# A decode layer on one core: PV with V as the stationary operand, whole last loads, and the FFN weights behind V

## The chip, the core and the metric

The kernel runs on one core of a Trainium2 chip. The metric is device microseconds (us) for one execution of the program. The engines named below are PE (TensorE matmul; PEld is its weight load), DVE (VectorE), ACT (ScalarE), POOL (GpSimd) and SP (SyncE, which here only issues DMAs). All DMAs of the core are carried out by 16 DMA engines.

## The reference

Two tokens (B = 2, one position each, D = 512) go through one transformer layer: attention over a cache of 8,192 positions with 32 heads of 128, and then a gated feed-forward network of width 1,376. Everything is bf16.

```python
def _A_ref(x, k_cache, v_cache, wq, wo):          # attention, 32 query and 32 KV heads
    q = (x @ wq).reshape(B, Sq, Hq, Dh).transpose(0, 2, 1, 3)
    scores = jnp.einsum("bhqd,bhkd->bhqk", q, k) * (Dh ** -0.5)
    p = _softmax(scores, axis=-1)
    o = jnp.einsum("bhqk,bhkd->bhqd", p, v)
    return o.transpose(0, 2, 1, 3).reshape(B, Sq, Hq * Dh) @ wo

def _B_ref(x, W_gate, W_up, W_down):
    gate = jnp.einsum("bsd,df->bsf", x, W_gate)
    up = jnp.einsum("bsd,df->bsf", x, W_up)
    gate = gate * (gate > 0)
    return jnp.einsum("bsf,fd->bsd", gate * up, W_down)

h = x + _A_ref(_layernorm(x), A_k_cache, A_v_cache, A_wq, A_wo)
h2 = h + _B_ref(_layernorm(h), B_W_gate, B_W_up, B_W_down)
```

The two caches are 2 x 32 x 8192 x 128 each, 134 MB in bf16, and every byte of them is read once: 268 MB of the 281 MB that the kernel loads.

## The kernel before

**Tiles.** The 64 (token, head) problems are worked on in NP = 32 pairs p of two heads of one token. For a pair, K is one tile of 128 partitions (two heads of 64) by J = 128 positions by 128 numbers, 4 MB in one transfer with 32 KB a row; V is the same. Four slots of that size hold K[p], V[p], K[p+1], V[p+1]; pair p's K is in slot 2p mod 4 and its V in slot 2p+1 mod 4.

**Scores of a pair** (loop at L399). Of the 128 positions of a partition, 96 are scored on DVE, in two parts c of 48: a product with the broadcast query (L407, 3.36 us), four halving additions (L415) and a reduction (L424). The other 32 are scored on PE: in four groups of eight they are transposed (L434) into one of two PSUM tiles Tp, copied to SBUF by ACT (L440), and multiplied with the query (L274). ACT makes the exponentials of the three pieces (L282) and their sums zs.

**PV of a pair** (`pv`, L341). For p < 31 the exp weights are the stationary operand: 8 columns (4 positions by 2 heads) are loaded, and 4 positions of V, 512 wide, move past them; 32 such matmuls (L361) sum into a bank of Op, in four groups of rows. `collect` (L368) then copies the bank to `os_sb` with ACT (L372) and picks the wanted pieces with four fp32 matmuls against a selection matrix `sel` into the bank `Ob` (L378; the trace shows each fp32 matmul as two). For the last pair V is the stationary operand, 128 by 128, and 2 columns of exp weights move (L354, 128 matmuls).

**Normalization.** After pairs 7, 15, 23 and 30, `z_sum` (L295) adds zs over partitions on PE, and `normalize` (L300) makes sums, reciprocals and the scaled O_sb on DVE. Batch 3 (pairs 24 to 30) is normalized in the middle of pair 31's DVE work (L418). Batch 4 is pair 31 alone.

**The end.** After the loop: `o_proj` (L328) of heads 24 to 31 that are ready, z_sum of batch 4, PV of pair 31, its scaling (`o_scale`), the last output projection, the layer norm, the two FFN input products (L518), their gate on DVE, the FFN output product (L560) and the result's DMA. These stand in a fixed order in each engine's program.

**Order of the work.** It is written by hand: every engine runs its instructions in program order, and waits on semaphore counts. All large loads are issued from SP's queue in this order: wq, K0, V0, K1, V1, the last rows of W_down, wo, then K[p+2] as soon as pair p has read its K (`t_kfree`), and V[p+2] as soon as PV of pair p is done. At the end the order is K30, K31, V30; then, when K30's slot is free, W_up and W_gate into it, V31 in four transfers of 1, 1.5, 1.25 and 0.25 MB with a semaphore each (`vparts`), and W_down. PE waits for both of W_up and W_gate at L512 and for all of W_down at L554.

## Time and profile before

| | us |
|---|---|
| time, median of 3 runs | 672.62 (672.58 to 673.44) |
| the profiled execution's own time | 672.58 |
| its span | 670.7 |
| PE busy, 3,868 matmuls | 352.0 |
| DVE busy | 494.4 |
| ACT busy | 220.1 |
| read from HBM | 281.05 MB, 419 GB/s over the span |
| DMA engines, packets of the data queue | 98.4% of the span |

Times in the profile run from the start of the span. The page gives busy time for each engine, the span in 40 slices with the busy share of each in tenths, the DMA queues, and the costliest groups of instructions with their source line (L12 is line 12). The chain that ended last follows the work back from the last instruction, at each step to what released it. The timeline lists instructions by time; a row with "x8" is eight merged instructions. A queue of the kind "instruction" carries the fetches of an engine's program, and one of the kind "hardware_dynamic" the kernel's own transfers. The trace also holds every DMA packet with queue, start, duration and size.

### The profile page before, as it was taken

Reading aid. Unit: us, or ns where it says so; the run is one execution under the profiler, and the core shown is the slowest. Engines: PE = TensorE matmul, PEld = TensorE weight load, DVE = VectorE, ACT = ScalarE, POOL = GpSimd, SP = SyncE. Lnnn points to the kernel's source line nnn. Section 1 sums busy time; section 2 is a strip of 40 time slices with the busy share of each in tenths; the row PEclk is TensorE's granted clock in tenths of the full one; section 3 lists DMA queues with packets and bytes.
Section 4 is the critical chain, followed back from the end, with each engine's and each line's share of the span. In section 5 each row is a group of like instructions: output and inputs, shape, how many; then the busy total and the mean of one; then the engine's idle time right before and its main releaser. Section 6 shows DMA issues by size and latency. Waiting matters only on the chain.

```text
span 670.7 us, 8986 instructions
## 1 busy us (share of the span) xinstructions
PE 352.0 (52%) x3868; PEld 234.1 (35%) x3868; DVE 494.4 (74%) x430; ACT 220.1 (33%) x554; POOL 2.5 (0%) x16
## 2 busy tenths in 40 slices
PE   2553355455545455554554655454556565455655
PEld 2431333233433223343322433232234443223435
DVE  1774477788768678877777887677786977678792
ACT  0631322233432234344222333322333342233340
POOL 1000000000000000000000000000000000000000
PEclk9999999665565555655556656655566555565555
DMA  9999999999999999999999999999999999999994
GB/s 375 434 436 357 434 435 430 427 431 429 434 433 427 428 433 433 425 436 425 434 433 427 431 436 424 431 432 431 437 426 425 434 432 433 426 430 431 428 409 146
DMA packets 15915, 281.63 MB, mean 420 GB/s; under 512 B 1442, under 2 KB 6916, under 8 KB 7044
## 3 DMA queue, kind: packets, MB, share of 16 engines
q1 hardware_dynamic: 15872, 281.06, 98.4%
q8 instruction: 30, 0.49, 0.3%
q14 instruction: 9, 0.07, 0.0%
q10 hardware_dynamic: 4, 0.00, 0.0%
HBM read 281.05 MB, written 0.00 MB: 419 GB/s over the span
## 4 chain that ended last, share of the span: by engine, by line
DMA 72%; DVE 22%; PE 3%; ACT 2%; issue 1%; SPq 0%; DVEq 0%
DMA slot<-in_A_k_cache_dram 68%; DVE prod L407 14%; DVE tb L415 4%; DMA slot<-in_A_v_cache_dram 3%; DVE prod L415 2%; ACT kT L440 1%; DVE scores L424 1%; PE T L434 1%; PE Ob L378 1%; ACT e L282 0%; PE S L274 0%; ACT os_sb L372 0%; PE Ob L295 0%; PE S L518 0%; PE O L560 0%
## 5 line engine op out<-in xcount | busy, mean ns | idle before, releaser
L407 DVE TENSOR_TENSOR prod<-slot,q_b 128x6144 bf16<-128x6144 bf16 x64 | 214.9, 3358 | 128.2 <-DMA slot<-in_A_k_cache_dram 126.9
L361 PE MATMUL O<-slot,e 128*8 128x512 bf16 x992 | 116.3, 621 | 143.4 <-ACT e L282 127.8
L440 ACT ACTIVATE kT<-T 128x1024 bf16<-128x1024 bf16 x128 | 126.2, 1021 | 160.2 <-PE T L434 159.4
L434 PE MATMUL T<-ident,slot 128*128 128x128 bf16 x1024 | 122.0, 305 | 65.3 <-DMA slot<-in_A_k_cache_dram 65.3
L415 DVE TENSOR_TENSOR tb<-prod 128x3072 bf16<-128x3072 bf16 (+1 forms) x128 | 148.2, 1158 | 4.4
L434 PEld LDWEIGHTS T<-ident,slot 128*128 128x128 bf16 x1024 | 99.3, 140 | 92.3 <-DMA slot<-in_A_k_cache_dram 90.6
L282 ACT ACTIVATE e<-scores 64x48 bf16<-64x48 f32 x128 | 32.8, 256 | 239.2 <-DVE scores L424 237.6
L361 PEld LDWEIGHTS O<-slot,e 128*8 128x8 bf16 x992 | 24.0, 106 | 209.6 <-ACT e L282 155.6
L415 DVE TENSOR_TENSOR prod<-tb 128x1536 bf16<-128x1536 bf16 (+1 forms) x128 | 84.2, 658 | 4.4
L378 PE MATMUL Ob<-sel,os_sb 128*128 128x2 f32 x248 | 57.5, 354 | 47.7 <-ACT os_sb L372 47.7
L378 PEld LDWEIGHTS Ob<-sel,os_sb 128*128 128x128 f32 x248 | 54.9, 327 | 51.2 <-ACT os_sb L372 51.2
L274 PE MATMUL S<-qT,kT 128*128 128x2 bf16 x1024 | 48.2, 168 | 39.2 <-ACT kT L440 38.1
L274 PEld LDWEIGHTS S<-qT,kT 128*128 128x128 bf16 x1024 | 40.7, 106 | 57.5 <-ACT kT L440 57.5
L424 DVE TENSOR_REDUCE scores<-prod 128x48 f32<-128x384 bf16 x64 | 35.4, 553 | 2.2
L282 ACT ACTIVATION_READ_ACCUMULATOR e<-scores 64x1 f32 x128 | 23.6, 185 | 0.0
L372 ACT ACTIVATE os_sb<-O 128x512 f32<-128x512 f32 x31 | 18.5, 597 | 3.4 <-PE O L361 2.7
L282 ACT ACTIVATE e<-S 64x32 bf16<-64x32 f32 x64 | 12.9, 202 | 15.0 <-PE S L274 14.2
L282 ACT ACTIVATION_READ_ACCUMULATOR e<-S 64x1 f32 x64 | 12.8, 201 | 0.7
L251 ACT ACTIVATE q_b<-O 128x512 bf16<-128x512 f32 x8 | 4.3, 595 | 15.8 <-PE O L246 15.8
L222 DVE CAST qT<-W 128x64 bf16<-128x64 f32 x1 | 0.2, 224 | 12.2 <-PE W L217 12.2
L217 PE MATMUL W<-xlT,X 128*128 128x2 bf16 x128 | 3.6, 166 | 8.8 <-DMA X<-in_A_wq_dram 8.8
L217 PEld LDWEIGHTS W<-xlT,X 128*128 128x128 bf16 x128 | 3.5, 104 | 8.8 <-DMA X<-in_A_wq_dram 8.8
(67 smaller groups left out, 58.8 us busy)
## 6 DMA issues: line engine op xcount, KB each, us to landing
slot<-in_A_k_cache_dram SPq DMA_DIRECT2D x32, 4096.0 KB, 27.7
slot<-in_A_v_cache_dram SPq DMA_DIRECT2D x31, 4096.0 KB, 31.3
X<-in_A_wq_dram SPq DMA_DIRECT2D x1, 4096.0 KB, 12.5
X<-in_A_wo_dram SPq DMA_DIRECT2D x1, 4096.0 KB, 48.7
slot<-in_A_v_cache_dram SPq DMA_DIRECT2D x1, 1536.0 KB, 19.8
slot<-in_B_W_up_dram SPq DMA_DIRECT2D x1, 1376.0 KB, 10.0
slot<-in_B_W_gate_dram SPq DMA_DIRECT2D x1, 1376.0 KB, 14.6
slot<-in_A_v_cache_dram SPq DMA_DIRECT2D x1, 1280.0 KB, 22.2
```

The costliest lines, as they stand in the source:

```text
L217: i = nc.tensor.matmul(Wp[:, h * B:(h + 1) * B], lhsT=wq[:, c, h * Dh:(h + 1) * Dh], rhs=lT[:, c * B:(c + 1) * B], start=(c == 0), stop=(c ...
L251: t_cp[m] = act.run(nc.scalar.activation(out=q_b[:, m * 512:(m + 1) * 512], in_=Op[m % 2][:], func=ACT.Copy))
L274: i = nc.tensor.matmul(Sp[p % 2][:, 2 * jj:2 * jj + 2], lhsT=kT[n % 3][:, k * 128:(k + 1) * 128], rhs=qT[:, 2 * p:2 * p + 2], start=True, ...
L282: t = act.run(nc.scalar.activation(out=e_t[p % 2][q, j0:j0 + nj, a], in_=src(q, a), func=ACT.Exp, scale=inv_sqrt_dh, accum_out=zs[q, 2 * p ...
L361: i = nc.tensor.matmul(o[g:g + 2 * VJ, :], lhsT=e_t[p % 2][:, j:j + VJ, :].rearrange("p j a -> p (j a)"), rhs=v_t[:, j:j + VJ, :].rearrang ...
L372: t_os[p] = act.run(nc.scalar.activation(out=os_sb[:], in_=Op[p % 2][:], func=ACT.Copy))
L378: i = nc.tensor.matmul(Ob[:, 2 * p:2 * p + 2], lhsT=os_sb[:, jj * Dh:(jj + 1) * Dh], rhs=sel[:, 2 * jj:2 * jj + 2], start=(jj == 0), stop= ...
L407: t_dm = dve.run(nc.vector.tensor_tensor(out=prod[:], in0=k_t[:, c * JC:(c + 1) * JC, :], in1=qv, op=ALU.mult))
L415: dve.run(nc.vector.tensor_tensor(out=o, in0=cur[:, :, 0:half], in1=cur[:, :, half:w], op=ALU.add))
L424: t_s = dve.run(nc.vector.tensor_reduce(out=sc[:], in_=cur, axis=AX.X, op=ALU.add))
L434: i = nc.tensor.transpose(Tp[n % 2][:, k * 128:(k + 1) * 128], k_t[:, j, :], ident[:])
L440: t_ev[n] = act.run(nc.scalar.activation(out=kT[n % 3][:], in_=Tp[n % 2][:], func=ACT.Copy))
```

## The change

The source is shorter by 49 lines. What it does:

- `pv` has one form for all pairs: 128 matmuls with V stationary and 2 columns of exp weights moving, straight into the pair's two columns of a bank of Op, which belongs to its batch. `collect`, `os_sb`, `sel`, the bank `Ob` and the zeroing of Op at the start are gone; z_sum follows the last PV of a batch and uses column 64 on of the same bank.
- The freed bank becomes a third transpose tile Tp.
- `pv(30)` and `normalize(3)` move behind the loop; before, they stood in the middle of pair 31's work on PE and DVE.
- V31 is one transfer, issued ahead of W_up and W_gate; W_up and W_gate have a semaphore each, and W_down comes in two parts (six and four blocks of 128 rows) with a semaphore each. PE waits for each where it needs it.

```diff
-    VJ = 4
+    WD_PARTS = ((0, 6), (6, 10))
...
-        Tp = [ps(f"T{i}", [128, GT * 128], BF16) for i in range(2)]
+        Tp = [ps(f"T{i}", [128, GT * 128], BF16) for i in range(3)]
...
-        Ob = ps("Ob", [128, 512], F32)
...
-                dve.wait(t_cp[NP // 4 - 2], t_cp[NP // 4 - 1])
-                for o in Op:
-                    t_zero = dve.run(nc.vector.memset(o[:], 0.0))
...
                 def zbank(k):
-                    return Sp[0] if k == 4 else Ob
+                    return Sp[0] if k == 4 else Op[k % 2]
...
                 def pv(p):
                     v_t = tile((2 * p + 1) % 4)
-                    o = Op[p % 2]
-                    parts = vparts if p == NP - 1 else (
-                        [(0, NCH * JC, J)] + [(1 + c, c * JC, (c + 1) * JC) for c in range(NCH)])
-                    pe.wait(t_zero)
-                    if p >= 2:
-                        pe.wait(t_os[p - 2])
+                    k = next(kk for kk, (a, b_) in enumerate(batches) if a <= p < b_)
+                    col = 2 * (p - batches[k][0])
+                    parts = [(0, NCH * JC, J)] + [(1 + c, c * JC, (c + 1) * JC) for c in range(NCH)]
+                    if p == batches[k][0] and k >= 2:
+                        pe.wait(t_O[k - 2])
                     nmm = 0
...
-                        for j in range(j0, j1, VJ):
-                            g = 32 * (nmm % 4)
+                    for ei, j0, j1 in parts:
+                        pe.wait(t_exp[p][ei], t_v[p])
+                        for j in range(j0, j1):
                             i = nc.tensor.matmul(
-                                o[g:g + 2 * VJ, :], lhsT=e_t[p % 2][:, j:j + VJ, :].rearrange("p j a -> p (j a)"),
-                                rhs=v_t[:, j:j + VJ, :].rearrange("p j d -> p (j d)"),
-                                start=(nmm < 4), stop=(nmm >= J // VJ - 4))
+                                Op[k % 2][:, col:col + 2], lhsT=v_t[:, j, :], rhs=e_t[p % 2][:, j, :],
+                                start=(nmm == 0), stop=(nmm == J - 1))
                             nmm += 1
                     t_pv[p] = pe.run(i)
-
-                def collect(p):
-                    act.wait(t_pv[p])
...
-                    t_os[p] = act.run(nc.scalar.activation(out=os_sb[:], in_=Op[p % 2][:], func=ACT.Copy))
...
-                    for jj in range(VJ):
-                        i = nc.tensor.matmul(
-                            Ob[:, 2 * p:2 * p + 2], lhsT=os_sb[:, jj * Dh:(jj + 1) * Dh],
-                            rhs=sel[:, 2 * jj:2 * jj + 2], start=(jj == 0), stop=(jj == VJ - 1))
-                    t_ob[p] = pe.run(i)
-                    if p + 1 in ends:
+                    if p + 1 in ends and p < NP - 1:
                         t_batch[k] = z_sum(k, *batches[k])
...
-                            if p == NP - 1 and c == 1 and w == Dh // 2:
-                                t_O[3] = normalize(3, 24, 31, t_batch[3], False)
...
-                                if n >= 2:
-                                    pe.wait(t_ev[n - 2])
+                                if n >= 3:
+                                    pe.wait(t_ev[n - 3])
...
-                            if p == NP - 1:
-                                pv(p - 1)
-                            if p >= 1:
-                                collect(p - 1)
...
                     elif p == NP - 2:
 
+                        load_v(p + 1)
                         sp.wait(*t_kfree[p])
                         for k, w in enumerate((B_W_up, B_W_gate)):
                             nc.sync.dma_start(
                                 slot[0][:, k * DC * F:(k + 1) * DC * F],
-                                w.rearrange("(p c) n -> p (c n)", c=DC)).then_inc(sem_w, 16)
-                        load_v(p + 1, vparts)
+                                w.rearrange("(p c) n -> p (c n)", c=DC)).then_inc(sem_w[k], 16)
+                        for k, (r0, r1) in enumerate(WD_PARTS):
+                            nc.sync.dma_start(
+                                slot[0][:, 2 * DC * F + r0 * D:2 * DC * F + r1 * D].rearrange("p (r n) -> p r n", n=D),
+                                B_W_down[r0 * 128:r1 * 128].rearrange("(r p) n -> p r n", p=128)).then_inc(sem_wd[k], 16)
...
+                pv(NP - 2)
+                t_O[3] = normalize(3, 24, 31, t_batch[3], False)
                 pe.wait(t_O[3])
                 o_proj(range(HM, 30), 0, 2)
...
-                pe.wait((sem_w, 32), t_d)
+                pe.wait(t_d)
...
+                pe.wait((sem_w[0], 16))
                 t_u = ffn_in(Sp[1], wup, 0, FC)
+                pe.wait((sem_w[1], 16))
                 t_g = (ffn_in(Op[1], wgt, 0, FH), ffn_in(Wp, wgt, FH, FC))
...
-                pe.wait((sem_wd, 32))
+                pe.wait((sem_wd[2], 16))
                 for k, (f0, f1) in enumerate(((0, FH), (FH, FC))):
-                    pe.wait(t_hd[k])
+                    pe.wait(t_hd[k], (sem_wd[k], 16))
```

## The prediction

> **What bounds the kernel now.** I read the page first, engines, slices and queues; then the chain that ended last, in order of time; then the timeline of the last 50 us; then the trace's DMA packets one by one.

> ```profile
> PE 352.0 (52%) x3868; PEld 234.1 (35%) x3868; DVE 494.4 (74%) x430; ACT 220.1 (33%) x554; POOL 2.5 (0%) x16
> DMA  9999999999999999999999999999999999999994
> q1 hardware_dynamic: 15872, 281.06, 98.4%
> q8 instruction: 30, 0.49, 0.3%
> L361 PE MATMUL O<-slot,e 128*8 128x512 bf16 x992 | 116.3, 621 | 143.4 <-ACT e L282 127.8
> L378 PE MATMUL Ob<-sel,os_sb 128*128 128x2 f32 x248 | 57.5, 354 | 47.7 <-ACT os_sb L372 47.7
> ```

> No compute engine is full; the DMA engines are, in every slice but the last. The kernel streams 281 MB, and K[p] and V[p] are 4 MB each. The fourth row will matter: 30 instruction fetches on a queue of their own, which use the same 16 DMA engines.

> The chain shows the beat at which K tiles arrive (start, length, what; DVE starts when K lands):

> ```profile
> 388.25 3.37 DVE prod L407
> ...
> 428.14 3.37 DVE prod L407
> ...
> 467.00 3.37 DVE prod L407
> ...
> 545.24 3.37 DVE prod L407
> ...
> 585.12 3.37 DVE prod L407
> ...
> 623.98 3.37 DVE prod L407
> ```

> Two pairs (four transfers) take 38.86 us, 9.715 us a transfer, except now and then: 388.25 to 428.14 is 39.89, 545.24 to 585.12 is 39.88. Something adds about 1 us to the slowest engine.

> The tail is the timeline (start, busy, engine, line):

> ```profile
> 652.36 0.19 DVE L303 TENSOR_REDUCE zr<-Ob 128x14 f32<-128x42 f32 x1
> 653.09 1.15 PEld L328 LDWEIGHTS W<-O_sb,X 128*128 128x128 bf16 x32 [1.59 <-DVE O_sb L316]
> 655.05 0.55 DVE L424 TENSOR_REDUCE scores<-prod 128x48 f32<-128x384 bf16 x1
> 656.38 0.50 PEld L295 LDWEIGHTS S<-zs,ones_f 128*128 128x128 f32 x2 [2.14 <-ACT e L282]
> 656.61 2.40 PEld L354 LDWEIGHTS O<-e,slot 128*128 128x128 bf16 x80
> 659.34 1.44 PE L354 MATMUL O<-e,slot 128*128 128x2 bf16 x48 [0.25 <-DMA slot<-in_A_v_cache_dram]
> 660.89 0.16 DVE L316 TENSOR_TENSOR O_sb<-O,zi 128x2 bf16<-128x2 f32 x1 [3.52 <-PE O L354]
> 662.41 1.53 PE L518 MATMUL S<-d_b,slot 128*128 128x2 bf16 x44 [0.34 <-DVE d_b L503]
> 665.24 1.48 PE L560 MATMUL O<-hd,slot 128*128 128x2 bf16 x40
> ```

> So the end is set twice, nearly at once: K30's landing (623.98) plus 31.6 us of uninterrupted DVE for pairs 30 and 31 gives the last scores at 655.60; and the last quarter-megabyte of V31 lands at 659.3. From 660.89 (o_scale) the rest is a fixed 9.8 us.

> **The steady state: instruction fetches.** The 30 packets of q8 have 16,384 bytes each. PE and PEld have 7,736 records, 258 a fetch, and the n-th fetch starts when the trace has passed about 256n of them (fetch 26 at 608.4 us, after 6,661): this queue feeds PE. Each 4 MB transfer leaves 16 completion writes of 4 bytes in the trace, one for each DMA engine. First and last of them for some transfers:

> ```
> first engine   last engine   lag     PE fetch just before
>    121.59        123.94      2.35    119.96 (5th)
>    218.71        222.11      3.40    215.71 (9th)
>    315.84        319.78      3.94    314.58 (13th)
>    412.97        417.95      4.98    407.91 (17th)
>    500.53        505.90      5.37    500.71 (21st)
>    578.24        584.65      6.41    578.24 (25th)
>    617.09        623.50      6.41    (this is K30)
> ```

> Engines that fetch nothing keep the 9.715 us beat. After a fetch one engine falls back by 1.53 to 1.56 us and never recovers, since all engines have a queue ahead of them. At K30 the 16 lags are six under 0.6, two at 2.8 and 4.0, six at 4.58 to 5.39 and two at 6.23 and 6.41. With 1.54 a hit, that is 6 x 3 + 2 x 4 = 26 hits, just the 26 fetches begun by then: they go round 8 engines. A transfer counts as landed when its slowest engine is done, so the worst-hit engine sets K30.

> What the change adds: for each of 31 pairs 128 matmuls in place of the 32 of L361 and the 8 of L378 (248/31), so 31 x 88 = 2,728 pairs of weight load and matmul; PE goes from 3,868 to 6,596 pairs, from 30 fetches to about 51. Up to K30's landing: 168 pairs of the prologue, 29 x 192, 64 of pair 29's transposes and scores, some 130 of its PV and 6 of z sums, about 5,936 pairs or 11,870 records: 46 fetches for 26. Round 8 engines 46 makes six engines with 6 hits and two with 5. The worst before has 4 hits and a lag of 0.25 besides (6.41 - 6.16); of the engines with 3 hits one has 0.77 besides (5.39 - 4.62), and by its turn (5th, 13th, ... 45th) it gets its sixth hit in time. New lag 6 x 1.54 + 0.77 = 10.0: K30 lands **3.6 us later**. Bounds: the first engine's two more hits alone 3.1; an average of 20 more fetches over 8 engines 3.85; a seventh hit on one engine 5.1 (9.24 + 0.77 + 1.54 - 6.41); nothing, if the extra fetches fall on engines with room. I take 3.6, as it follows the same count that closes before.

> [...]

> **The rest of the steady state costs nothing.** PV of one pair on PE: 32 wide matmuls took 3.58 us (timeline, 645.00) and the L378 group 1.87; 128 narrow pairs at 2.40/80 = 30 ns take 3.84. ACT loses the 0.60 us copy of L372. PE's total of about 9.2 us a pair lies under a beat of 19.4. K[p+2] is issued 11.1 us after K[p] lands (604.54 to 615.68), V[p+2] after pv(p), some 18 us after, with three transfers of 9.7 us still queued, so neither delay is seen. At the three batch ends normalize now follows pv(p) directly: exps end 16.1 us after K's landing, 48 pairs 1.4, z_sum 0.6, three DVE operations 0.8, done at 19.0 of 19.4. The start drops two memsets (1.03 us, L257) and POOL's copies, covered by K2, which is not issued before 35.96 and then waits in the queue. PE's third transpose bank only loosens a wait.

> **The tail, step by step, relative to K30.** normalize(3) leaves the middle of pair 31's DVE work (the gap 652.45 to 653.07, less the usual 0.03: -0.59), so the last scores come at 655.01. It now runs behind them, 0.68 us (652.36 to 653.04), ready 655.69; queued behind it on DVE is only normalize(4), while PE's o_proj and everything after wait for it. 32 o_proj pairs (1.15 us) start 655.74; z_sum's first load to PV's first is 0.23 (656.38 to 656.61), so PV31 loads from 657.1. All 128 pairs now stand behind this point: 3.84 us, matmuls done about 661.05. Before, they ended 660.78. That is **+0.27**: the wait for V31's last part goes, and 48 more pairs plus o_proj come in its place. At the nearest slower row (L274: 8 in 0.38, 47 ns, pipeline fill included) it would be +2.4; at the prologue's 3.57/128 = 28 ns under a granted clock of 1.00, against 0.50 in the tail, about -0.3 over PV and FFN. I keep L354's own 30 ns. pv(30), moved behind pair 31's scores (done 645.1), needs 3.84 us and a z_sum, over by 650 at the old time, 5 us before normalize wants it.

> DMA order: V31 goes ahead of W_up and W_gate as one issue for four, W_down as two for one. V31's wait for pv(29) (done 622.2) now stands in SP's queue ahead of the wait for K30's slot (635.11), so it holds nothing back. V31 lands at 633.70 (K31) + 2 x 9.715 + 3.6 = 656.7, needed at 660.7. The weights then take 3.26, 3.26 and 3.04 us at 432 GB/s: 660.0, 663.2, 666.3 against uses at 666.3, 667.7 and 669.1. Same bytes, nothing late. The split waits on PE thus all fall on landed data.

> **Sum:** profiled execution 672.58 (span 670.7, 1.9 around it) + 3.6 + 0.27 = 676.45, +0.57%. The median of the runs shown is 672.62, the same within 0.04, so **676.4**.

> **Rivals.** (A) The fetches do not move K30: hidden, or dealt out over other engines in the longer program. Price +0.27 alone: **672.9**, not slower within what can be told (0.2%, 1.35 us, is about what a measurement of this kernel can tell from no change). It decides as long as K30 lands before 625.1. For: the prologue of the ring is not in the trace, and a fetch is only 0.3% of the DMA time. Against: 26 hits counted out of 26 fetches. Faster would need over 1.6 us from landings; a spread over 16 engines (3 hits for 4) would give 1.0 less, 671.9. (B) One more turn: a seventh hit, or the same worst engine also takes an 8 KB fetch of the other engines' queue (9 in the run, 0.7 to 1.0 us each): K30 +5.1, **678.0**; the weights' slack of 2.8 us is then nearly used as well, and past it W_down's second part, now the last transfer, sets the end. For: PE's burst of some 300 pairs in the tail draws three or four fetches there. Against: the count of 46. (C) PE as the new bound, with 128 weight loads a pair at 47 ns, 6.0 us: still 11.4 of 19.4 a pair, but +2.4 in the tail, 672.58 + 3.6 + 2.4 = **678.6**. Against: L354 has 128 of these very pairs.

> **How the numbers follow.** Forecast 0.74, A 0.12, B and C together 0.14. The likeliest gives 676.4. The range runs from 674.5 (one hit less on the worst engine, 3.6 - 1.54 = 2.1, and the tail's +0.27 taken back by the faster row) to 678.6 (C, with B inside); A stays outside. Slower: forecast, B and C, 0.88, less a little for hits that miss K30, 0.86; A gives 0.10 of no change and 0.04 of faster.

> **What would show it.** The q8 row with about 51 packets; lags of first to last engine of about 10 us at K30; the first prod of pair 30 at 627.6; the base beat still 38.86 per two pairs; o_scale of the last batch 36.9 to 37.3 us after K30's landing; no wait of PE for V31 or a weight. Wrong, if q8 grows and K30 stays at 624, if PV31 spaces its pairs over 35 ns, or if PE stalls on its own instructions.

## The result, and the profile after

The changed kernel takes 676.11 us (median of 4, 675.81 to 676.30) where the kernel before takes 672.79 (median of 4): a ratio of 1.0047 with an interval of 1.003 to 1.0065, slower by 3.3 us. The profiled execution took 675.94 us with a span of 674.2, against 672.58 and 670.7.

The page of the changed kernel, its engines, its slices and its DMA queues:

```profile
PE 294.7 (44%) x6596; PEld 266.7 (40%) x6596; DVE 493.6 (73%) x428; ACT 202.2 (30%) x523; POOL 1.7 (0%) x11
DMA  9999999999999999999999999999999999999993
q1 hardware_dynamic: 15456, 281.06, 97.9%
q8 instruction: 51, 0.84, 0.5%
L333 PE MATMUL O<-e,slot 128*128 128x2 bf16 x4096 | 118.5, 165 | 236.9 <-ACT e L268 119.0
```

PE is less busy than before (294.7 us for 352.0), and so is ACT. The bytes are the same. What has grown is the row that looks like nothing: 51 instruction fetches for 30, and PE's count of pairs, 6,596 for 3,868.

The chain in order of time, as before with the first product of every second pair (start, length, what):

```profile
429.71 3.37 DVE prod L359
...
470.11 3.37 DVE prod L359
...
508.95 3.37 DVE prod L359
...
549.33 3.37 DVE prod L359
...
588.18 3.37 DVE prod L359
...
627.01 3.37 DVE prod L359
```

The undisturbed beat is the same: 508.95 - 470.11 = 38.84, 588.18 - 549.33 = 38.85. The long steps are 40.40 and 40.38, 1.5 us over the beat. By the last completion writes of the 4 MB transfers from V4 to K30 there are five such steps, of 1.4 to 1.55 us, where the kernel before has six, of 0.5 or 1.0: they are not more frequent but larger. Pair 30 starts at 627.01 instead of 623.98.

The timeline of the tail (start, busy, engine, line):

```profile
657.49 0.55 DVE L374 TENSOR_REDUCE scores<-prod 128x48 f32<-128x384 bf16 x1
657.96 0.19 DVE L286 TENSOR_REDUCE zr<-O 128x14 f32<-128x42 f32 x1
658.69 1.15 PEld L310 LDWEIGHTS W<-O_sb,X 128*128 128x128 bf16 x32 [6.83 <-DVE O_sb L298]
660.00 3.68 PEld L333 LDWEIGHTS O<-e,slot 128*128 128x128 bf16 x128
663.87 0.16 DVE L298 TENSOR_TENSOR O_sb<-O,zi 128x2 bf16<-128x2 f32 x1 [3.11 <-PE O L333]
665.29 0.50 PE L467 MATMUL S<-d_b,slot 128*128 128x2 bf16 x13 [0.26 <-DVE d_b L452]
666.22 1.18 PE L467 MATMUL S<-d_b,slot 128*128 128x2 bf16 x31 [0.42 <-issue]
668.70 1.48 PE L511 MATMUL O<-hd,slot 128*128 128x2 bf16 x40
```

From K30's landing to o_scale it is 663.87 - 627.01 = 36.86 us, before 36.91: the tail neither gained nor lost there. No wait for V31 or for a weight is left. But the FFN's 44 matmuls, one run before, are cut in two: PE stands still at 665.6, for "issue", that is for nothing the profile shows. From o_scale to the FFN's output product it is 4.83 us instead of 4.35. So the 3.46 us by which the last DVE operation is later (670.43 against 666.97) are 3.03 from K30, -0.05 from the attention's tail and 0.48 from the FFN.

### The profile page after: what moved, and what is told of

Same layout as the page of the kernel before. It is cut to its first block, busy times and chain, and to the rows that moved or that the text cites. A ratio compares the mean times of both kernels' runs of the same rounds, so it can differ in the third digit from the quotient of the medians.

```text
span 674.2 us, 14429 instructions
## 1 busy us (share of the span) xinstructions
PE 294.7 (44%) x6596; PEld 266.7 (40%) x6596; DVE 493.6 (73%) x428; ACT 202.2 (30%) x523; POOL 1.7 (0%) x11
## 3 DMA queue, kind: packets, MB, share of 16 engines
q1 hardware_dynamic: 15456, 281.06, 97.9%
## 4 chain that ended last, share of the span: by engine, by line
DMA 70%; DVE 27%; PE 2%; issue 1%; SPq 0%; DVEq 0%
DMA slot<-in_A_k_cache_dram 70%; DVE prod L359 16%; DVE tb L367 6%; DVE prod L367 4%; DVE scores L374 2%; PE O L333 1%; PE S L467 0%; PE W L310 0%; PE O L511 0%; SPq L136 0%; PE W L467 0%; PE O L467 0%; PE S L278 0%; SPq L152 0%; DVE O_sb L298 0%
## 5 line engine op out<-in xcount | busy, mean ns | idle before, releaser
L333 PE MATMUL O<-e,slot 128*128 128x2 bf16 x4096 | 118.5, 165 | 236.9 <-ACT e L268 119.0
L333 PEld LDWEIGHTS O<-e,slot 128*128 128x128 bf16 x4096 | 114.4, 104 | 241.1 <-ACT e L268 121.5
L260 PE MATMUL S<-qT,kT 128*128 128x2 bf16 x1024 | 48.3, 168 | 38.6 <-ACT kT L390 37.3
L310 PE MATMUL W<-O_sb,X 128*128 128x2 bf16 (+1 forms) x136 | 5.0, 172 | 7.0 <-DVE O_sb L298 7.0
L310 PEld LDWEIGHTS W<-O_sb,X 128*128 128x128 bf16 x136 | 4.8, 118 | 7.2 <-DVE O_sb L298 7.2
```

The costliest lines, as they stand in the source:

```text
L260: i = nc.tensor.matmul(Sp[p % 2][:, 2 * jj:2 * jj + 2], lhsT=kT[n % 3][:, k * 128:(k + 1) * 128], rhs=qT[:, 2 * p:2 * p + 2], start=True, ...
L310: i = nc.tensor.matmul(Wp[:, c * B + b0:c * B + b1], lhsT=wo_m[:, h, c, :], rhs=Ov[:, h // 2, h % 2, b0:b1], start=first[0], stop=last, sk ...
L333: i = nc.tensor.matmul(Op[k % 2][:, col:col + 2], lhsT=v_t[:, j, :], rhs=e_t[p % 2][:, j, :], start=(nmm == 0), stop=(nmm == J - 1))
```

## The experiments

They ran in two sets, each on one chip and beside the kernel before: new order alone, old order, 91 and 182 matmuls more beside a median of 673.03 us, the other four beside 672.91. The ratios are to these medians. Two questions stood open: is it the number of PE's instructions, or the narrow weight loads of V, or the new order of the last loads; and what bounds the tail.

### The order of the last loads alone

```diff
-                        pe.wait(t_exp[p][ei], (sem_vl[ci], 16) if p == NP - 1 else t_v[p])
+                        pe.wait(t_exp[p][ei], t_v[p])
...
+                        load_v(p + 1)
                         sp.wait(*t_kfree[p])
...
-                        load_v(p + 1, vparts)
```

> The kernel before with one part of the change alone: V31 as one transfer ahead of W_up and W_gate; PV stays 512 wide. Fetch theory: PE's program is the same, so 30 fetches, lag at K30 6.4 us, first prod of pair 30 at 624.0. PV31 no longer waits for V31: 128 pairs at 29 to 30 ns behind 656.6, o_scale at 660.4 to 660.6 for 660.89, so 672.2 to 672.4 us. Rival (the new order of the last loads is what costs): 675.5 to 676.5 us.

Measured: 672.23 us (11 executions, ratio 0.9989, 0.9981 to 0.9998), 0.8 under the kernel before. Its timeline, from PV31's weight loads to o_scale:

```profile
656.85 3.68 PEld L354 LDWEIGHTS O<-e,slot 128*128 128x128 bf16 x128
...
660.72 0.16 DVE L316 TENSOR_TENSOR O_sb<-O,zi 128x2 bf16<-128x2 f32 x1 [3.11 <-PE O L354]
```

The 128 pairs now run without the break that V31's third part made, 28.75 ns each in the mean. K30 landed as before (624.20). The new order is no cost but a gain of 0.1%.

### The changed kernel with the old order

```diff
-                        load_v(p + 1)
                         sp.wait(*t_kfree[p])
...
+                        for ci, (_, j0, j1) in enumerate(vparts):
+                            nc.sync.dma_start(...).then_inc(sem_vl[ci], 16)
```

> The changed kernel with the load order of before (W_up, W_gate, V31 in four parts, W_down). Fetch theory: 51 fetches, lag at K30 9.7 us, first prod of pair 30 at 627.0; V31's last part lands near 662.3, PV31 is done near 663.8, as in the changed kernel: 675.6 to 676.6 us. Rival (the load order is what costs): 672.5 to 673 us, with K30 at 624.

Measured: 677.11 us (ratio 1.0058, 1.0045 to 1.0072). K30 came at 627.41, as the theory has it, but the time lies above its band, because V31 came later than expected.

```profile
660.42 2.40 PEld L336 LDWEIGHTS O<-e,slot 128*128 128x128 bf16 x80
664.50 1.44 PE L336 MATMUL O<-e,slot 128*128 128x2 bf16 x48 [1.60 <-DMA slot<-in_A_v_cache_dram]
```

The 80 pairs are V31's first two parts; PE then waits 1.6 us for the third, of 1.25 MB, until 664.50, 5.2 later than in the kernel before (659.34) and not 3. Its 16 completion writes show why: fifteen come within 5.61 us of the first, and one comes 7.14 behind it, so one engine had taken another fetch by then (the one at 652.89). With so many fetches, V31 behind the weights is the next thing to be late, and the new order hides that.

### As many instructions, with the old PV

```diff
                     t_pv[p] = pe.run(i)
+                    if p < NP - 2:
+                        for _ in range(91):
+                            nc.tensor.matmul(Ob[:, 256:258], lhsT=ident[:], rhs=ident[:, 0:2],
+                                             start=True, stop=True)
```

Ob's columns 256 and 257 are read by nothing.

> The kernel before with 91 more matmuls on PE after the PV of each of the pairs 0 to 29 (identity by two of its columns into an unused place of Ob): as many PE instructions as the changed kernel, with V still read 512 wide, ACT's copy, and the old load order. Fetch theory: 51 or 52 fetches, lag at K30 9.4 to 10.0 us, first prod of pair 30 at 627.0 to 627.6, tail as before: 675.5 to 676.3 us. Rivals (the narrow PV's weight loads of V slow the DMA or PE; the load order): 672.4 to 673.0 us, first prod at 624.

Measured: 677.66 us (ratio 1.0068, 1.0056 to 1.0081). Its queue row, and its timeline at pair 30's first product and at PV31:

```profile
q8 instruction: 51, 0.84, 0.5%
```

```profile
627.27 3.36 DVE L411 TENSOR_TENSOR prod<-slot,q_b 128x6144 bf16<-128x6144 bf16 x1 [3.94 <-DMA slot<-in_A_k_cache_dram]
...
664.46 1.44 PE L354 MATMUL O<-e,slot 128*128 128x2 bf16 x48 [1.63 <-DMA slot<-in_A_v_cache_dram]
```

Neither PV nor the loads were changed, and K30 lands 3.3 us late all the same, at the changed kernel's place, with the changed kernel's 51 fetches. The time is 1.4 us over the band's end for the reason seen in the run before: V31's third part is late once more in the old order (664.46).

### The same, with the new order

```diff
+                        load_v(p + 1)
                         sp.wait(*t_kfree[p])
...
-                        load_v(p + 1, vparts)
...
+                        for _ in range(91):
+                            nc.tensor.matmul(Ob[:, 256:258], lhsT=ident[:], rhs=ident[:, 0:2], ...)
```

> The kernel before with the new order of the last loads and the 91 more matmuls a pair, but V still read 512 wide. Fetch theory: K30 at 627.0 to 627.4 as with 91 alone, and V31, now ahead of the weights, no longer waited for: o_scale 36.5 us behind K30, 675.2 to 675.9 us, about 2 less than with the old order. Rival (the extra 1.5 to 2 us of the run with 91 alone came from the added matmuls themselves, not from V31's place): 677 to 678 us.

Measured: 676.07 us (ratio 1.0047, 1.0034 to 1.006). This is the changed kernel's time (676.11, ratio 1.0047) with PV 512 wide, `collect` and the old normalize in place: instruction count and load order alone give all of it, within the intervals. o_scale is 36.5 us behind K30 (663.79 - 627.29), as expected. It is just over the band because its FFN has PE's pause too:

```profile
665.30 0.81 PE L522 MATMUL S<-d_b,slot 128*128 128x2 bf16 x25 [0.35 <-DVE d_b L507]
...
666.72 0.88 PE L522 MATMUL S<-d_b,slot 128*128 128x2 bf16 x19 [0.61 <-issue]
```

### Twice the dose

The same edit as with 91, with 182 in its place and the old order.

> The same with 182 more matmuls a pair, twice the dose. Fetch theory: 72 to 73 fetches, 68 of them by K30's landing, 8 or 9 on each of 8 engines, lag 9 x 1.54 + 0.3 to 0.5 = 14.1 to 14.4 us, first prod of pair 30 7.7 to 8.0 us later than before, 680.0 to 681.0 us. Rival (fetches are hidden): 672.4 to 673.0 us. If the lag is bounded by the queue's depth: between 676 and 680.

Measured: 682.80 us (680.55 to 683.18, ratio 1.0138). There were 73 fetches, and pair 30 started at 631.65, 7.7 us later than before: the dose holds for K30's landing. The lag did not reach 14 us at K30. It was 9.54 at K20 and 11.26 at K24, and then only 5.42, because the fastest engines came late as well (626.21 for 617.56): they had run out of issued transfers. The first engine was done with everything before K26 at 529.98, but SP issued K26 only at 531.80; for K27 it was 552.99 and 555.42. K26's slot comes free with a DVE product that stands behind a normalize, and this waited 7.90 us for PE's z_sum, where it waits 2.06 in the kernel before (516.14):

```profile
527.68 0.21 DVE L303 TENSOR_REDUCE zr<-Ob 128x16 f32<-128x48 f32 x1 [7.90 <-PE Ob L295]
```

The hits still add up: of the eight engines that take PE's fetches, three come 5.29 to 5.42 us behind the first at K30 and five 3.77 to 4.21, one hit less, and 3 x 9 + 5 x 8 = 67. The time is about 2 us over the band, and the reason is the place of the extra work: with 182 matmuls behind the PV of pair 29, pair 30's z_sum was late and DVE stood 3.24 us before normalize(3).

```profile
663.36 0.20 DVE L303 TENSOR_REDUCE zr<-Ob 128x14 f32<-128x42 f32 x1 [3.24 <-PE Ob L295]
```

### Half of the narrow loads

```diff
+                    nall = J if p == NP - 1 else J // 2
...
-                        for j in range(j0, j1):
+                        for j in range(j0, j1, 1 if p == NP - 1 else 2):
...
-                                start=(nmm == 0), stop=(nmm == J - 1))
+                                start=(nmm == 0), stop=(nmm == nall - 1))
```

> The changed kernel with every second of the 128 matmuls left out in the PV of pairs 0 to 30 (half of the positions are not summed), so 64 narrow weight loads of V a pair and 4,612 matmuls in all. Fetch theory: 35 fetches, 31 or 32 by K30's landing, 4 hits on most of 8 engines, lag 6.5 to 7.0 us, first prod of pair 30 at 624.0 to 624.6, tail as in the changed kernel: 672.4 to 673.6 us. Rival (each narrow load of V costs the DMA time in proportion): half of the changed kernel's +3.0, first prod at 625.5.

Measured: 672.86 us (11 executions, ratio 1.0000, 0.9991 to 1.0009). Its queue row and pair 30's first product:

```profile
q8 instruction: 36, 0.59, 0.4%
```

```profile
624.02 3.36 DVE L360 TENSOR_TENSOR prod<-slot,q_b 128x6144 bf16<-128x6144 bf16 x1 [3.96 <-DMA slot<-in_A_k_cache_dram]
```

Still 64 weight loads of V a pair, but the program is short again: 36 fetches, K30 at 624.02, no later than before. Not half of the loss is left but none, as counted hits have it: 32 fetches by then are 4 on each of 8 engines, and the kernel before had 4 on its worst.

### The lags, run by run

All this is one table (the medians of the first and fourth kernel are those of the first section). It goes by the completion writes of K30's transfer, sorted by their semaphore, so that writes of neighbouring transfers can't mix (the lag of the kernel before is then 6.39, where the prediction read 6.41):

```
                     PE pairs  fetches (by K30)  first done  last done   lag   pair 30   median us
before                  3,868      30 (26)         617.56      623.95    6.39   623.98   672.79
new order alone         3,868      30 (26)         617.38      624.18    6.80   624.20   672.23
half of the loads       4,612      36 (32)         617.42      624.00    6.58   624.02   672.86
changed kernel          6,596      51 (47)         617.24      626.98    9.75   627.01   676.11
changed, old order      6,596      51 (47)         617.66      627.39    9.73   627.41   677.11
91 more                 6,598      51 (47)         617.50      627.24    9.74   627.27   677.66
91 more, new order      6,598      51 (47)         617.59      627.26    9.67   627.29   676.07
182 more                9,328      73 (67)         626.21      631.62    5.42   631.65   682.80
```

Rows with 26 or 32 fetches have K30 at 624, rows with 47 at 627, whatever PV and load order are. In the changed kernel seven lags are 9.50 to 9.75 and one is 8.22: with 1.54 a hit that is 7 x 6 + 5 = 47, again each fetch accounted for.

### A shorter tail

The last scores are 31.6 us behind K30 in the kernel before, all of it DVE's work, and PE has time there. So, on top of the new order, the last two pairs give more positions to PE, W_up, W_gate and the two parts of W_down have a semaphore each, and normalize(3) stands behind the loop. The main lines of the edit:

```diff
+    def jp(p):
+        return JPL if p >= NP - 2 else JP
+    def jc(p):
+        return (J - jp(p)) // NCH
...
-                            if p == NP - 1 and c == 1 and w == Dh // 2:
-                                t_O[3] = normalize(3, 24, 31, t_batch[3], False)
...
+                t_O[3] = normalize(3, 24, 31, t_batch[3], False)
                 pe.wait(t_O[3])
```

with JPL 48 in one run and 64 in the other.

> The kernel before with the new order of the last loads, W_down in two parts, and for pairs 30 and 31 alone 48 positions scored on PE and 80 on DVE instead of 32 and 96; normalize(3) stands behind the loop. If the tail is bound by DVE behind K30: scores end at 650.2 instead of 655.6, PV31 starts when V31 lands (near 653), and then the last weights bind (W_down's second part near 662.9): 669.5 to 670.5 us. Rival (the tail is bound by something that comes after the scores): 672 us.

> The same with 64 positions on PE and 64 on DVE for the last two pairs. If the last weights bind in both: within 0.3 us of the version with 48. If DVE still binds there: 1 to 2 us faster than it. If ACT and PE, which copy and transpose twice as much, have become the bound: slower than it.

Measured: 670.16 us with 48 (ratio 0.9958, 0.9945 to 0.9972), which beats both kernels, and 671.00 with 64 (0.9969, 0.9957 to 0.998; 669.9 to 671.94). The timeline with 48:

```profile
650.00 0.49 DVE L432 TENSOR_REDUCE scores<-prod 128x40 f32<-128x320 bf16 x1
...
653.29 3.58 PE L363 MATMUL O<-e,slot 128*128 128x2 bf16 x128 [0.21 <-DMA slot<-in_A_v_cache_dram]
...
659.43 1.46 PE L528 MATMUL S<-d_b,slot 128*128 128x2 bf16 x41 [0.72 <-issue]
...
663.36 0.67 PE L571 MATMUL O<-hd,slot 128*128 128x2 bf16 x16 [0.22 <-DMA slot<-in_B_W_down_dram]
```

The scores end 5.1 us earlier, PV31 starts as V31 lands, and the last matmuls now wait for the last bytes of W_down. The kernel is back at its DMA stream, and a faster way to the last 16 matmuls can't be worth more. (This is the profiled execution, of 669.51 us, the fastest of the five.)

64 positions are not the near tie expected if the last weights bind in both: 0.84 us slower in the medians. The trace of its fastest execution shows the third case of the expectation, PE and ACT as the bound: DVE's scores are done at 646.30, and normalize(3) waits for PE.

```profile
651.66 0.20 DVE L313 TENSOR_REDUCE zr<-Ob 128x14 f32<-128x42 f32 x1 [5.37 <-PE Ob L305]
```

PV31 then starts at 653.93 instead of 653.29, and the FFN's output at 662.40 instead of 662.20. This doesn't give the whole 0.84, and the larger spread of the times was not explained.

## Why the prediction was right, step by step

The forecast was 676.4 us, slower, and 676.11 was measured.

**Fetches and hits** were the right cause. The profile had 51 packets as forecast, and the runs with added matmuls show that PE's count moves K30 with nothing else changed. The count by K30 was 47, not 46, which makes seven engines with six hits instead of six.

**K30's landing** was forecast 3.6 us later and came 3.03 later. Of the 0.57 between them, 0.26 is a mis-sized term, the 0.77 that was added for the engine of the 5th, 13th, ... fetch: the largest lag over 6 x 1.54 was 0.51. The other 0.3 is that the first engine was done 0.32 us earlier than before (617.24 for 617.56), which the step did not foresee. The lower bound of 3.1, from two more hits alone, was the better one.

**PV in the steady state at nothing** held: the same time with PV 512 wide and as many instructions. One reason given for it was too generous: three transfers were not always still queued ahead when one was issued. In the changed kernel the first engine was done with K30 at 617.24, before K31 was issued at about 619, and its K31 came 13.02 us later instead of 9.71. It cost nothing, as the slowest engine always had work (K31's last write came 9.72 us after K30's), but it is the same running dry that the run with 182 shows earlier.

**The tail**, +0.27 to o_scale, was -0.05: relative to K30, PV31 started 0.13 us earlier than forecast and took 3.68 us, not 3.84. The 30 ns were the mean of a row of 80 pairs with its start in it. Between two weight loads it is 0.21 us once, at the start, and then 26.7 ns, in PV31 of both kernels; in one row of 128 the start counts once, and the mean is 28.75. The prologue's 28 ns is such a mean too: its pairs (128 from 13.00 us on in the changed kernel) also follow each other at 26.7 ns, and the granted clock was 1.00 there (0 to 17 us), for 0.50 in the tail (660 to 674): the pairs came no faster at the higher one. Also, the wait at 659.34 in the kernel before was for V31's third part, of 1.25 MB, which landed at 659.30; the last quarter-megabyte landed at 659.93, and no wait for it shows. That normalize(3) and 48 more pairs would use up what the missing wait for V31 gives was right in kind. What the step left out is that the wait would have grown: with the old order V31 is 1.6 us late in the longer program, so the new order is worth more there (with 91 more matmuls it takes the kernel from 4.6 to 3.2 us over the kernel before) than in the short one (0.8).

**PE's pauses** came in the changed kernel: the prediction's own sign, "if PE stalls on its own instructions", came true. In the dense tail the pause cost 0.48 us, where the kernel before runs the same 44 matmuls in one piece (1.53 us from 662.41). In the stream PE once stood still as well, 2.5 us at 529.8, where it had time to spare (the last section has the row). That the forecast came within 0.3 us is partly luck: -0.57 at K30 and -0.32 to o_scale stand against +0.48 in the FFN, for which the sum had no term.

**Rival A**, fetches that don't move K30, fell with the run of 91 matmuls. **B**, a seventh hit, did not come by K30; one came by V31 (one engine 1.56 us behind the next, V31 landed at 657.70) and cost nothing, as PE first uses V31 at 660.00. **C**, weight loads at 47 ns, fell with the 28.75 ns.

## What to carry to other kernels

## What the runs showed of the hardware

PE's pauses in the tails have one place. Counting PE's records in the trace from the start (matmuls, weight loads and its own waits), each pause in the tails comes where the count passes 193 + 256 k, in different lines of code, and each ends 1.38 to 1.49 us after an instruction fetch has ended:

```
                      record   pause from   to        fetch          fetch's end to next record
changed kernel        12,993     665.63    666.22   663.71 - 664.74      1.48
half of the loads      9,153     664.56    665.07   662.60 - 663.69      1.38
91 more, new order    12,993     665.94    666.71   664.15 - 665.23      1.49
48 on PE               7,617     658.54    659.43   656.88 - 657.98      1.45
64 on PE               7,873     661.07    661.55   659.10 - 660.16      1.38
before (no pause)      7,617     664.38    664.39   661.82 - 662.92      1.46
```

At the other places of this kind, among the last three of each of the ten traces, the fetch had ended 1.77 us or more before the record, and there is no pause. In the stream of the kernel before one such place, record 5,313 at 502.67, has the end of a fetch only 0.85 us before it and no pause. The changed kernel's stream has one such pause, at record 10,177, behind the 96 matmuls of an output projection that follow the end of a PV at once. It ends 1.41 us after the fetch of 529.82 to 530.93:

```profile
532.34 1.87 PE L384 MATMUL T<-ident,slot 128*128 128x128 bf16 x16 [2.51 <-issue]
```

In 46 of 50 places of the changed kernel, and in 14 of 29 of the kernel before, the next fetch starts 2.6 to 4.2 us after such a record. Take the pause in the changed kernel's tail: from record 12,737 at 660.88 to the packet's start at 663.71 are 2.8 us, the packet takes 1.0, and PE goes on 1.5 us later, 5.3 us in all, while 256 records of narrow pairs take 3.4 (128 at 26.7 ns). Part of the 2.8 us may be time behind the stream's packets, an estimate from one fetch: in the kernel before, the last one, after the last load had landed (663.27), started 0.94 us after its record (664.38 to 665.32). Why PE pauses at these places was not shown: no run moves a place or a fetch by itself. At record 7,617 of the kernel before the next record stands 1.46 us behind the fetch's end without a pause.
